# Attention scores in batches of three head pairs, one of them in the output projection's banks, with buffers of one pair

## The chip, the cores and the metric

The kernel runs on one core of a Trainium2 chip. The metric is the device time of one execution in microseconds. The engines of the core work in parallel, each with its own program in order, and wait for one another through semaphores: TensorE (PE; its weight loads are listed apart as PEld), VectorE (DVE), ScalarE (ACT), GpSimd (POOL), and SyncE (SP), which here only issues DMA transfers. TensorE writes to PSUM, which has eight banks of 512 fp32 columns.

## The reference

All tensors are bf16: 2048 tokens of width 640, 32 heads of 192, and a window of the last 512 keys and values. The expert part (B) touches only the two best tokens.

```python
xn = _layernorm(x, axis=-1)
q  = (xn @ wq).reshape(B, Sq, 32, 192)             # heads
scores = einsum("bhqd,bhkd->bhqk", q, k) * 192 ** -0.5   # 512 keys of each head
p  = softmax(scores);  o = einsum("bhqk,bhkd->bhqd", p, v)
s  = o.reshape(B, Sq, 32 * 192) @ wo
# B: r = xn @ w_r picks 2 tokens; their gated FFN, times sigmoid(r), is added to xn there
g  = silu(xn with the two updated rows)
return x + s * g
```

## The kernel before

The heads are taken in 8 groups of four, a group's heads in two pairs. A *step* is a group, a block of 512 tokens (`t5`) and a pair of heads: 64 steps. A *quad* `k` is half a step, 256 tokens of a pair, that is two tiles of 128 tokens (`u`) with two heads each: 128 quads, and 256 *pairs* (a tile of 128 tokens with two heads). For every pair of heads the 384 rows of q and k are three chunks of 128: chunk 0 belongs to the first head, chunk 2 to the second, and chunk 1 holds the last 64 rows of each.

The order of all engines is that in which the program issues the instructions. For the first twelve quads it is written out by hand in a list of tokens (`FIRST`), for the last in another (`LAST`); between them a loop (L797) lays down, for each quad `k`:

- `quad(k)`: scores of two tiles into four PSUM banks (`ps_sc`). First four matmuls with 128 rows (L296, L297: chunks 0 and 2), then four with 64 rows (L302, L303: chunk 1, one head in the upper half of the array and one in the lower);
- four row maxima on VectorE (`row_max`, L314) and four exponentials on ScalarE (`exps`, L321), which also sum each row; then one DMA transpose of the 128x2048 exponentials, pexp to pT (L327, 16 blocks of 128x128);
- the q products of the next step (`q_item`, L263), evicted by ScalarE (L268);
- the o products of quad `k - 2` (`o_products`, L339; two items, one for each tile), scaled on VectorE by the reciprocal sums (L353), and after the second one DMA transpose of the 128x768 o_sb to oT (L357, 6 blocks);
- one item of the output projection (`w_item`) for a tile of tokens that is complete, six quads later: six matmuls of 512 columns (L386) and six of 128 (L388) into one tile of two banks (`ps_w`), added to `s_acc` by VectorE (L394);
- pieces of other work by quad number (`mid` and `bg`): loads of the next group's weights, keys and values, issued by SyncE, the transposes of keys (L125, 12 blocks), the expert's part, and the final load of x (L780).

PSUM holds two banks for q and o products (`ps_f`), two for w and four for scores. Buffers rotate: two of pexp and four of pT, each for a quad, two of o_sb, three of oT. All DMA transposes are on SyncE's queue.

LayerNorm of the first 512 tokens uses ScalarE's square root; for the others VectorE computes 1 / deviation by three Newton steps (`rsqrt_newton`, L182), and the row statistics with `bn_stats` (L418).

The functions that the diff touches, and what calls them, with the profile's line numbers:

Of the kernel before, what the change touches and what calls it, by code (L numbers as in the profile page):

```python
# [21 lines left out]
def kernel(ctx, tc, A_x, A_k_cache, A_v_cache, A_wq, A_wo, B_x, B_w_r, B_w_gate, B_w_up, B_w_down, out):  # L22
# [45 lines left out]
    p_pool = pool("p", 2)  # L68
    pT_pool = pool("pT", 4)
    o_pool = pool("o", 2)  # L70
    oT_pool = pool("oT", 3)
# [70 lines left out]
    warm_ps = ps_w.tile([P, W], FP32, name="warm_ps", tag="w_ps")  # L142
# [62 lines left out]


# [17 lines left out]
    def k_turn(copies):  # L224

        grp[0]["kT"] = kT_pool.tile([P, PAIRS, NJ, 3, P], BF16, name="kT")
        tp = ps_w.tile([P, NJ * 3, P], BF16, name="tp_k", tag="w_ps")
        kp = grp[0][("k", 0)].rearrange("p j h d -> p (j h d)")
        kT = grp[0]["kT"][:, 0].rearrange("p j c t -> p (j c) t")
        step = NJ * 3 // len(copies)  # L230
        for c in range(NJ * 3):
            nc.tensor.transpose(out=tp[:, c, :], in_=kp[:, c * P:(c + 1) * P], identity=ident)
        for q, copy in enumerate(copies):
            cs = slice(q * step, (q + 1) * step)
            copy(out=kT[:, cs], in_=tp[:, cs])
# [10 lines left out]
    NH = 2 * NS  # L246
# [3 lines left out]
    pe_of = {}  # L250
# [34 lines left out]
    def quad(k):  # L285
        i, hf = divmod(k, 2)
        g, t5, pr = steps[i]
        qT = qT_of[i]
        kT = grp[g]["kT"]
        kp = kT[:, pr]  # L290
        tiles = []
        for u in range(2):
            ssl = slice((2 * hf + u) * P, (2 * hf + u + 1) * P)
            s0 = ps_sc.tile([P, W], FP32, name="s0", tag="sc")
            s1 = ps_sc.tile([P, W], FP32, name="s1", tag="sc")
            nc.tensor.matmul(s0, lhsT=qT[:, 0, ssl], rhs=kp[:, :, 0, :], start=True, stop=False)  # L296
            nc.tensor.matmul(s1, lhsT=qT[:, 2, ssl], rhs=kp[:, :, 2, :], start=True, stop=False)  # L297
            tiles.append((s0, s1))
        for u in range(2):
            ssl = slice((2 * hf + u) * P, (2 * hf + u + 1) * P)  # L300
            s0, s1 = tiles[u]
            nc.tensor.matmul(s0, lhsT=qT[0:64, 1, ssl], rhs=kp[0:64, :, 1, :], start=False, stop=True)  # L302
            nc.tensor.matmul(s1, lhsT=qT[64:128, 1, ssl], rhs=kp[64:128, :, 1, :], start=False, stop=True)  # L303
        return tiles
# [3 lines left out]
    def row_max(k, tiles, c):  # L308
        if c == 0:
            nm_of[k] = small.tile([P, 4], FP32, name="nm")  # L310
            l_of[k] = small.tile([P, 4], FP32, name="lsum", bufs=6)
            pT_of[k] = pT_pool.tile([P, 2, 2, NJ, P], BF16, name="pT")
            pe_of[k] = p_pool.tile([P, 2, 2, W], BF16, name="pexp")
        nc.vector.tensor_reduce(out=nm_of[k][:, c:c + 1], in_=tiles[c // 2][c % 2], axis=AX.X, op=ALU.max, negate=True)  # L314

    def exps(k, u, tiles):
        pexp = pe_of[k]
        nm = nm_of[k]
        for hh in range(2):
            c = 2 * u + hh  # L320
            nc.scalar.activation(out=pexp[:, u, hh, :], in_=tiles[u][hh], func=ACT.Exp, bias=nm[:, c:c + 1],  # L321
                                 scale=1.0, accum_out=l_of[k][:, c:c + 1])
        if k >= NH - 2:
            nc.sync.dma_start_transpose(out=pT_of[k][:, u].rearrange("p h j t -> p (h j) t"),
                                        in_=pexp[:, u].rearrange("p h k -> p (h k)"))
        elif u == 1:
            nc.sync.dma_start_transpose(out=pT_of[k].rearrange("p u h j t -> p (u h j) t"),  # L327
                                        in_=pexp.rearrange("p u h k -> p (u h k)"))

    def recip(k):  # L330
        nc.vector.reciprocal(out=l_of[k], in_=l_of[k])

    def o_products(k, u):
        i, hf = divmod(k, 2)
        g, t5, pr = steps[i]
        o_ps = f_tile([P, 2, Dh], FP32, "o_ps")
        for hh in range(2):
            for j in range(NJ):
                nc.tensor.matmul(o_ps[:, hh, :], lhsT=pT_of[k][:, u, hh, j, :], rhs=grp[g]["v"][:, 2 * pr + hh, j, :],  # L339
# [3 lines left out]
    def o_scaled(k, u, o_ps, act=False):  # L343
        i, hf = divmod(k, 2)
# [566 lines left out]
```

## Time and profile before

| | us |
|---|---|
| median of 3 runs | 814.38 |
| lowest, highest | 813.56, 817.44 |
| the profiled execution | 815.97 |
| its span | 814.2 |
| PE busy in the span | 796.1 |
| DVE busy | 625.4 |
| ACT busy | 485.6 |
| POOL busy | 208.2 |

Lines of the profile name the source line, the engine, the operation, output and inputs, tile sizes and a count; then the busy time and the mean of one in ns; then idle time of the engine before such instructions and what ended most of it. SyncE has no row of busy time: its entries are seen in its timeline, "SPq", with the time that one took. In a timeline a row that stands for several instructions carries the time from the first's start to the last's end.

### The profile page before, as it was taken

What the parts mean: (1) busy time and instruction counts of PE and PEld (TensorE: products, weight loads), DVE (VectorE), ACT (ScalarE), POOL (GpSimd) and SP (SyncE); (2) the same over time, 40 slices, a digit from 0 to 9 for tenths busy, and PEclk for the clock granted to TensorE, in tenths of its full rate; (3) what the DMA queues carried; (4) which work ended last, traced back from release to release, by engine and by line L of the source; (5) the groups of instructions that cost most, each with busy time, mean ns of one, the idle gap of its engine ahead of it and who ended that gap; (6) DMA issues with size and microseconds to landing.
All of it is one profiled execution on the core that took longest, in us unless ns stands there. A gap on an engine that the chain in (4) does not pass through costs nothing. (4 is left out here: it accounts for less than half of the span.)

```text
span 814.2 us, 15365 instructions
## 1 busy us (share of the span) xinstructions
PE 796.1 (98%) x5715; PEld 446.1 (55%) x5782; DVE 625.4 (77%) x1249; ACT 485.6 (60%) x1271; POOL 208.2 (26%) x157
## 2 busy tenths in 40 slices
PE   8889999999999999999999999999999999999997
PEld 4455555555555555555555555555555555555555
DVE  7988688887778777677776776777888877767886
ACT  5677666565566556555655565666776765655652
POOL 0001000000000000000001799999920001452533
PEclk9999999999999999999999999999999999999999
DMA  7988999989989999999999999788998879988884
GB/s 233 170 161 170 187 173 192 174 158 191 158 165 163 188 199 191 183 189 180 201 190 193 174 172 195 154 145 148 189 177 151 158 145 197 198 156 156 179 159 117
DMA packets 440555, 142.09 MB, mean 175 GB/s; under 512 B 413572, under 2 KB 440072, under 8 KB 440480
## 3 DMA queue, kind: packets, MB, share of 16 engines
q1 hardware_dynamic: 438720, 138.26, 89.9%
q0 software_dynamic: 816, 2.03, 1.0%
q8 instruction: 45, 0.74, 0.4%
q10 hardware_dynamic: 944, 0.82, 0.3%
q14 instruction: 30, 0.25, 0.1%
HBM read 39.98 MB, written 2.62 MB: 52 GB/s over the span
## 5 line engine op out<-in xcount | busy, mean ns | idle before, releaser
L321 ACT ACTIVATE pexp<-s,nm 128x512 bf16<-128x512 f32 x512 | 348.3, 691 | 253.8 <-DVE nm L314 163.4
L314 DVE TENSOR_REDUCE nm<-s 128x1 f32<-128x512 f32 x512 | 319.0, 683 | 55.2 <-PE s L303 55.2
L263 PE MATMUL q_ps<-xnT,wq_g 128*128 128x512 bf16 x945 | 234.9, 380 | 0.6 <-DMA xnT<-xn 0.6
L339 PE MATMUL o_ps<-v_sb,pT 128*128 128x192 bf16 x2048 | 210.3, 246 | 2.3 <-DMA pT<-pexp 0.8
L339 PEld LDWEIGHTS <-pT 128*128 128x128 bf16 x2048 | 173.0, 98 | 49.5 <-issue 5.8
L353 DVE TENSOR_TENSOR o_sb<-o_ps,lsum 128x384 bf16<-128x384 f32 x248 | 135.2, 545 | 47.2 <-PE o_ps L339 47.1
L386 PE MATMUL w_ps<-wo_g,oT 128*128 128x512 bf16 x662 | 163.4, 379 | 3.4
L263 PEld LDWEIGHTS <-wq_g 128*128 128x128 bf16 x945 | 80.2, 98 | 119.6 <-issue 50.1
L268 ACT ACTIVATE qT<-q_ps 128x512 bf16<-128x512 f32 x185 | 109.9, 596 | 40.8 <-PE q_ps L263 40.6
L394 DVE TENSOR_TENSOR s_acc<-s_acc,w_ps 128x640 f32<-128x640 f32 x96 | 78.9, 821 | 61.5 <-PE w_ps L388 61.4
L321 ACT ACTIVATION_READ_ACCUMULATOR pexp<-s,nm 128x1 f32 x512 | 106.3, 208 | 0.0
L386 PEld LDWEIGHTS <-oT 128*128 128x128 bf16 x726 | 69.1, 98 | 57.1
L297 PE MATMUL s<-kT,qT 128*128 128x512 bf16 x256 | 97.0, 379 | 1.9 <-ACT pexp L321 1.2
L296 PE MATMUL s<-kT,qT 128*128 128x512 bf16 x256 | 97.1, 379 | 0.6 <-ACT pexp L321 0.6
L303 PE MATMUL s<-kT,qT 64*128 64x512 bf16 x256 | 77.1, 381 | 0.0
L302 PE MATMUL s<-kT,qT 64*128 64x512 bf16 x256 | 77.1, 381 | 0.0
L388 PEld LDWEIGHTS <-oT 128*128 128x128 bf16 x726 | 50.7, 98 | 28.6
L725 POOL TENSOR_SCALAR yh<-y_bc,oh 128x640 bf16<-128x640 bf16 x32 | 60.3, 1884 | 3.4 <-DMA y_bc<-y_d 1.9
L388 PE MATMUL w_ps<-wo_g,oT 128*128 128x128 bf16 x726 | 60.3, 219 | 0.0
L711 POOL DMA_DIRECT2D y<-yp x4 | 2.1, 530 | 219.4 <-DMA oT<-o_sb 219.4
L726 POOL TENSOR_TENSOR xn<-xn,yh 128x640 bf16<-128x640 bf16 x32 | 44.7, 1396 | 2.7
L302 PEld LDWEIGHTS <-qT 64*128 64x128 bf16 x256 | 14.1, 94 | 56.3 <-issue 56.3
(135 smaller groups left out, 388.6 us busy)
## 6 DMA issues: line engine op xcount, KB each, us to landing
wo_g<-in_A_wo_dram SPq DMA_DIRECT2D x48, 160.0 KB, 2.9
wq_g<-in_A_wq_dram SPq DMA_DIRECT2D x35, 192.0 KB, 3.0
k_raw<-in_A_k_cache_dram SPq DMA_DIRECT2D x32, 192.0 KB, 3.1
v_sb<-in_A_v_cache_dram SPq DMA_DIRECT2D x32, 192.0 KB, 2.8
x_fin<-in_A_x_dram SPq DMA_DIRECT2D x16, 160.0 KB, 2.7
pT<-pexp SPq DMA_TRANSPOSE x130, 4.8
oT<-o_sb SPq DMA_TRANSPOSE x126, 3.2
wgu<-in_B_w_gate_dram SPq DMA_DIRECT2D x15, 128.0 KB, 2.9
```

The lines of the kernel that those rows point to most:

```text
L263: nc.tensor.matmul(q_ps, lhsT=grp[g]["wq"][:, dc, col0:col0 + P], rhs=xnT[:, t5 * 4:(t5 + 1) * 4, dc, :], start=(dc == 0), stop=(dc == DC ...
L268: nc.scalar.activation(out=qT_of[i][:, c, :], in_=q_ps, func=ACT.Copy, scale=scale)
L296: nc.tensor.matmul(s0, lhsT=qT[:, 0, ssl], rhs=kp[:, :, 0, :], start=True, stop=False)
L297: nc.tensor.matmul(s1, lhsT=qT[:, 2, ssl], rhs=kp[:, :, 2, :], start=True, stop=False)
L302: nc.tensor.matmul(s0, lhsT=qT[0:64, 1, ssl], rhs=kp[0:64, :, 1, :], start=False, stop=True)
L314: nc.vector.tensor_reduce(out=nm_of[k][:, c:c + 1], in_=tiles[c // 2][c % 2], axis=AX.X, op=ALU.max, negate=True)
L321: nc.scalar.activation(out=pexp[:, u, hh, :], in_=tiles[u][hh], func=ACT.Exp, bias=nm[:, c:c + 1], scale=1.0, accum_out=l_of[k][:, c:c + 1])
L339: nc.tensor.matmul(o_ps[:, hh, :], lhsT=pT_of[k][:, u, hh, j, :], rhs=grp[g]["v"][:, 2 * pr + hh, j, :], start=(j == 0), stop=(j == NJ - 1))
L353: nc.vector.tensor_tensor(out=o_sb[:, u], in0=o_ps, in1=l_of[k][:, 2 * u:2 * u + 2].unsqueeze(2).to_broadcast([P, 2, Dh]), op=ALU.mult)
L386: nc.tensor.matmul(w_ps[:, 0:DA], lhsT=oT[:, c // 3, u % 2, c % 3, :], rhs=wo_g[:, c, 0:DA], start=(c == 0), stop=(c == CPG - 1))
L388: nc.tensor.matmul(w_ps[:, DA:D], lhsT=oT[:, c // 3, u % 2, c % 3, :], rhs=wo_g[:, c, DA:D], start=(c == 0), stop=(c == CPG - 1))
L394: nc.vector.tensor_tensor(out=s_acc[:, n, :], in0=s_acc[:, n, :], in1=w_ps, op=ALU.add)
```

## The change

The unit of work becomes the pair. Buffers of pexp, pT, o_sb and oT hold one pair each (4, 6, 3 and 14 of them), and each pair has DMA transposes of its own: 128x1024 of exponentials, 128x384 of o. After the first twelve units, which are quads as before, a unit is three pairs: `scores(U)` issues six matmuls with 128 rows and then six with 64 rows. Two of the three pairs go to the four banks of `ps_sc`, the first pair to the two banks of the output projection (`w_banks`), which are two tiles of one bank now. The last unit is one pair. `w_item` computes two halves of 320 columns, one in each bank, with an eviction each.

The loop's order is a list (`STRETCH`), with o products one unit behind their scores. `FIRST` and `LAST` are written anew. For later tokens, 1 / deviation comes from ScalarE's Ln and Exp and one Newton step (`rsqrt_parts`), for four of the tiles of tokens (those that `FIRST` lists with `sa`) the row statistics come from ScalarE sums (`rows`), and a table set with both functions is loaded where a warming Exp stood.

The core of the diff:

```diff
-    p_pool = pool("p", 2)
-    pT_pool = pool("pT", 4)
-    o_pool = pool("o", 2)
-    oT_pool = pool("oT", 3)
+    p_pool = pool("p", 4)
+    pT_pool = pool("pT", 6)
+    o_pool = pool("o", 3)
+    oT_pool = pool("oT", 14)
...
+    def rsqrt_parts(var_ap, out_ap):
+
+        T = {}
+
+        def ln():
+            T["v"] = small.tile([P, 4], FP32, name="nw_v")
+            T["a"] = small.tile([P, 4], FP32, name="nw_a")
+            nc.scalar.activation(out=T["a"], in_=var_ap, func=ACT.Ln, bias=eps_t[:, 0:1], scale=1.0)
+
+        def ex():
+            nc.scalar.activation(out=out_ap, in_=T["a"], func=ACT.Exp, scale=-0.5)
+
+        def v():
+            nc.gpsimd.tensor_scalar(out=T["v"], in0=var_ap, scalar1=EPS, scalar2=None, op0=ALU.add)
+
+        def s1():
+            nc.vector.scalar_tensor_tensor(out=T["a"], in0=out_ap, scalar=-0.5, in1=out_ap, op0=ALU.mult, op1=ALU.mult)
+
+        def s2():
+            nc.vector.tensor_tensor(out=T["a"], in0=T["a"], in1=T["v"], op=ALU.mult)
+
+        def s3():
+            nc.vector.scalar_tensor_tensor(out=out_ap, in0=T["a"], scalar=1.5, in1=out_ap, op0=ALU.add, op1=ALU.mult)
+        return [ln, ex, v, s1, s2, s3]
...
+    HEAD = 12
+    units = [[2 * k, 2 * k + 1] for k in range(HEAD)]
+    while units[-1][-1] < NM - 2:
+        units.append([units[-1][-1] + 1 + a for a in range(3)])
+    units.append([NM - 1])
+    NU = len(units)
...
+    def w_banks():
+
+        if not wb:
+            wb.extend(ps_w.tile([P, W], FP32, name=f"w_{c}", tag=f"w{c}") for c in range(2))
+        return wb
+
+    def scores(U):
+
+        ms = units[U]
+        tiles = {}
+        for m in ms[1:] + ms[:1] if len(ms) == 3 else ms:
+            g, t5, pr = steps[m // 4]
+            ssl = slice((m % 4) * P, (m % 4 + 1) * P)
+            if len(ms) == 3 and m == ms[0]:
+                s0, s1 = w_banks()
+            else:
+                s0 = ps_sc.tile([P, W], FP32, name="s0", tag="sc")
+                s1 = ps_sc.tile([P, W], FP32, name="s1", tag="sc")
+            qT, kp = qT_of[m // 4], grp[g]["kT"][:, pr]
             nc.tensor.matmul(s0, lhsT=qT[:, 0, ssl], rhs=kp[:, :, 0, :], start=True, stop=False)
             nc.tensor.matmul(s1, lhsT=qT[:, 2, ssl], rhs=kp[:, :, 2, :], start=True, stop=False)
-            tiles.append((s0, s1))
-        for u in range(2):
-            ssl = slice((2 * hf + u) * P, (2 * hf + u + 1) * P)
-            s0, s1 = tiles[u]
+            tiles[m] = (s0, s1)
+        for m in ms:
+            g, t5, pr = steps[m // 4]
+            ssl = slice((m % 4) * P, (m % 4 + 1) * P)
+            s0, s1 = tiles[m]
+            qT, kp = qT_of[m // 4], grp[g]["kT"][:, pr]
             nc.tensor.matmul(s0, lhsT=qT[0:64, 1, ssl], rhs=kp[0:64, :, 1, :], start=False, stop=True)
             nc.tensor.matmul(s1, lhsT=qT[64:128, 1, ssl], rhs=kp[64:128, :, 1, :], start=False, stop=True)
-        return tiles
+        return [tiles[m] for m in ms]
 
     nm_of = {}
 
-    def row_max(k, tiles, c):
+    def row_max(U, tiles, c):
         if c == 0:
-            nm_of[k] = small.tile([P, 4], FP32, name="nm")
-            l_of[k] = small.tile([P, 4], FP32, name="lsum", bufs=6)
-            pT_of[k] = pT_pool.tile([P, 2, 2, NJ, P], BF16, name="pT")
-            pe_of[k] = p_pool.tile([P, 2, 2, W], BF16, name="pexp")
-        nc.vector.tensor_reduce(out=nm_of[k][:, c:c + 1], in_=tiles[c // 2][c % 2], axis=AX.X, op=ALU.max, negate=True)
-
-    def exps(k, u, tiles):
-        pexp = pe_of[k]
-        nm = nm_of[k]
+            nm_of[U] = small.tile([P, 6], FP32, name="nm")
+            l_of[U] = small.tile([P, 6], FP32, name="lsum", bufs=6)
+        nc.vector.tensor_reduce(out=nm_of[U][:, c:c + 1], in_=tiles[c // 2][c % 2], axis=AX.X, op=ALU.max, negate=True)
...
+    def exps(U, a, tiles):
+        m = units[U][a]
+        unit_of[m] = (U, a)
+        pT_of[m] = pT_pool.tile([P, 2, NJ, P], BF16, name="pT")
+        pexp = p_pool.tile([P, 2, W], BF16, name="pexp")
...
+            c = 2 * a + hh
+            nc.scalar.activation(out=pexp[:, hh, :], in_=tiles[a][hh], func=ACT.Exp, bias=nm_of[U][:, c:c + 1],
+                                 scale=1.0, accum_out=l_of[U][:, c:c + 1])
+        nc.sync.dma_start_transpose(out=pT_of[m].rearrange("p h j t -> p (h j) t"), in_=pexp.rearrange("p h k -> p (h k)"))
...
+    def o_scaled(m, o_ps, act=False, turn=True):
+        U, a = unit_of[m]
+        o_of[m] = o_pool.tile([P, 2, Dh], BF16, name="o_sb")
+        oT_of[m] = oT_pool.tile([P, 3, P], BF16, name="oT")
+        ls = l_of[U][:, 2 * a:2 * a + 2]
         if act:
             for hh in range(2):
-                nc.scalar.activation(out=o_sb[:, u, hh], in_=o_ps[:, hh, :], func=ACT.Copy, scale=l_of[k][:, 2 * u + hh:2 * u + hh + 1])
+                nc.scalar.activation(out=o_of[m][:, hh], in_=o_ps[:, hh, :], func=ACT.Copy, scale=ls[:, hh:hh + 1])
         else:
-            nc.vector.tensor_tensor(out=o_sb[:, u], in0=o_ps, in1=l_of[k][:, 2 * u:2 * u + 2].unsqueeze(2).to_broadcast([P, 2, Dh]), op=ALU.mult)
-        if pr == 0 and u == 0:
-            oT_of[(g, t5, hf)] = oT_pool.tile([P, PAIRS, 2, 3, P], BF16, name="oT")
-        if u == 1 and k < NH - 2:
-            nc.sync.dma_start_transpose(out=oT_of[(g, t5, hf)][:, pr].rearrange("p u c t -> p (u c) t"),
-                                        in_=o_sb.rearrange("p u h d -> p (u h d)"))
-
-    def o_item(k, u, act=False):
-        return lambda: o_scaled(k, u, o_products(k, u), act)
-
-    def o_turn(k):
-
-        i, hf = divmod(k, 2)
-        g, t5, pr = steps[i]
-        tp = tail_banks[0].tile([P, 2, 3, P], BF16, name="tp_o", tag="t")
-        for u in range(2):
-            o2 = o_of[k][:, u].rearrange("p h d -> p (h d)")
+            nc.vector.tensor_tensor(out=o_of[m], in0=o_ps, in1=ls.unsqueeze(2).to_broadcast([P, 2, Dh]), op=ALU.mult)
+        if turn:
+            nc.sync.dma_start_transpose(out=oT_of[m], in_=o_of[m].rearrange("p h d -> p (h d)"))
...
+    def w_products(b, u, w_ps, part, off=0):
+
+        wo_g = grp[steps[b * PAIRS][0]]["wo"]
+        for c in range(CPG):
+            nc.tensor.matmul(w_ps[:, part.start - off:part.stop - off], lhsT=oT_of[8 * b + 4 * (c // 3) + u][:, c % 3, :],
+                             rhs=wo_g[:, c, part], start=(c == 0), stop=(c == CPG - 1))
...
+            for h, w_ps in enumerate(w_banks()):
+                cs = slice(h * HD, (h + 1) * HD)
+                w_products(b, u, w_ps, cs, cs.start)
+                if g == 0 and act:
+                    nc.scalar.copy(out=s_acc[:, n, cs], in_=w_ps[:, 0:HD])
+                elif g == 0:
+                    nc.vector.tensor_copy(out=s_acc[:, n, cs], in_=w_ps[:, 0:HD])
+                elif g < NG - 1:
+                    nc.vector.tensor_tensor(out=s_acc[:, n, cs], in0=s_acc[:, n, cs], in1=w_ps[:, 0:HD], op=ALU.add)
+                else:
+                    if h == 0:
+                        t = fin_pool["t"].tile([P, D], FP32, name="fin_t")
+                        o = fin_pool["o"].tile([P, D], BF16, name="fin_o")
+                    nc.vector.tensor_tensor(out=t[:, cs], in0=w_ps[:, 0:HD], in1=xn[:, n, cs], op=ALU.mult)
...
-            nc.scalar.activation(out=const.tile([P, 1], FP32, name="warm"), in_=eps_t, func=ACT.Exp)
+            nc.scalar.preload_act_table_set("natural_log_exp_and_others")
...
+    STRETCH = "M0 M1 R O1 E0 q1 M2 M3 E1 O1 M4 M5 E2 W1 m q1 n W q O b".split()
...
+    for U in range(HEAD, NU - 2):
+        ms = units[U]
+        qs = [q_item(*divmod(n, 3)) for n in range(nq, q_until(U - HEAD))]
+        nq += len(qs)
+        os_ = [o_item(m) for m in range(no, ms[0])]
+        no += len(os_)
+        ws = []
+        while 12 + 2 * nw <= ms[-1]:
+            ws.append(w_item(*divmod(nw, 4)))
+            nw += 1
+        ks = [m // 2 for m in ms if m % 2 == 0]
+        todo = {"q": qs, "O": os_, "W": ws, "m": mid.pop(ks[0], []), "b": bg.pop(ks[-1], []),
+                "n": bg.pop(ks[0], []) + mid.pop(ks[-1], []) if len(ks) > 1 else []}
+        tiles = scores(U)
+        for token in STRETCH:
+            if token[0] == "M":
+                row_max(U, tiles, int(token[1]))
+            elif token[0] == "E":
+                exps(U, int(token[1]), tiles)
+            elif token[0] == "R":
+                if U > HEAD:
+                    recip(U - 1)
+            elif token[1:] == "":
+                while todo[token]:
+                    todo[token].pop(0)()
+            else:
+                for f in todo[token[0]][:int(token[1])]:
+                    todo[token[0]].pop(0)()
+        assert not any(todo.values())
```

## The prediction

> **What bounds the kernel now.** I read the page first, then the windows by stage, then the timeline of TensorE and of SyncE in the middle of the run, then the views of SyncE's transposing lines. The page:
>
> ```profile
> span 814.2 us, 15365 instructions
> PE 796.1 (98%) x5715; PEld 446.1 (55%) x5782; DVE 625.4 (77%) x1249; ACT 485.6 (60%) x1271; POOL 208.2 (26%) x157
> PE   8889999999999999999999999999999999999997
> L302 PEld LDWEIGHTS <-qT 64*128 64x128 bf16 x256 | 14.1, 94 | 56.3 <-issue 56.3
> ```
>
> TensorE is the bound. Only the first slices show holes. The last line counts 128 stops (one per batch of scores) before the 64-row weights. The timeline shows what a stop is:
>
> ```profile
> 403.12 0.38 PE L297 MATMUL s<-kT,qT 128*128 128x512 bf16 x1
> 403.44 0.39 PE L302 MATMUL s<-kT,qT 64*128 64x512 bf16 x1
> 403.44 0.39 PE L303 MATMUL s<-kT,qT 64*128 64x512 bf16 x1
> 403.66 0.38 PE L302 MATMUL s<-kT,qT 64*128 64x512 bf16 x1
> 403.67 0.38 PE L303 MATMUL s<-kT,qT 64*128 64x512 bf16 x1
> 403.97 1.25 PE L263 MATMUL q_ps<-xnT,wq_g 128*128 128x512 bf16 x5
> ```
>
> Matmuls of 512 columns start 0.215 us apart. From the last 128-row score to the first 64-row one it is 0.32, and from the last 64-row one to the next product 0.31: 0.10 + 0.09 = 0.19 us lost per batch, on the path.
>
> The second resource is not in the page's busy rows: SyncE, which issues every transpose and nearly every load in order. Its timeline where it has no pause:
>
> ```profile
> 304.84 2.91 SPq L327 DMA_TRANSPOSE pT<-pexp  x1
> 307.85 1.23 SPq L357 DMA_TRANSPOSE oT<-o_sb  x1
> 309.13 0.57 SPq L120 DMA_DIRECT2D wo_g<-in_A_wo_dram  x1
> 309.75 1.31 SPq L626 DMA_DIRECT2D wgu<-in_B_w_gate_dram  x2
> 311.17 2.91 SPq L327 DMA_TRANSPOSE pT<-pexp  x1
> ```
>
> The next instruction begins 0.05 us after a transpose ends, or 0.10 if it is a transpose (a separate wait instruction stands between). An entry starts only after its data is there: the pT at 573.24, after a pause of 1.2 us, begins just as ScalarE has read out the sum of its batch's last exponential. So these durations hold no waiting for data; in them SyncE can do nothing else. How they go with size (min/median/max ns):
>
> ```profile
> L327 SPq DMA_TRANSPOSE pT<-pexp x126: 1317/2536/4295, 18.4 to 786.5; - x126
> ...
> L125 SPq DMA_TRANSPOSE kT<-k_raw x15: 1279/1922/3092, 10.1 to 689.5; - x15
> ...
> L324 SPq DMA_TRANSPOSE pT<-pexp x4: 1232/1240/1302, 790.6 to 797.1; - x4
> ...
> L357 SPq DMA_TRANSPOSE oT<-o_sb x126: 1212/1273/2653, 31.1 to 799.0; - x126
> ```
>
> These are 16, 12, 8 and 6 blocks of 128x128. The minima are nearly one number: 1.15 us for the instruction and 0.0105 us per block. What the median of 16 blocks has above its minimum is waiting for the DMA engines to drain.
>
> **The change part by part.**
>
> *Batches of three.* Batches go from 128 to 90 (12 of two pairs, 77 of three, 1 of one). 38 x 0.19 = 7.2 us less on TensorE. The count of matmuls for scores, q and o stays.
>
> *w in halves.* These rows are its price on TensorE:
>
> ```profile
> 806.29 1.79 PE L859 MATMUL w_t<-wo_g,oT 128*128 128x512 bf16 x12
> 807.92 1.79 PE L859 MATMUL w_e<-wo_g,oT 128*128 128x320 bf16 x12
> ```
>
> The first is six matmuls of 512 and six of 128, the second twelve of 320: the same 1.79 us, so nothing. On VectorE an eviction goes from 0.82 us to two of 0.49 (the row fin_t<-w_e): +0.16 x 121 = 19 us, hidden, since VectorE is busy 77%.
>
> *The w banks shared with scores.* A w product now waits until a pair's exponentials have left those two banks, and scores of the next batch wait until w is evicted. Walked from the first score at 0, with row maxima 0.60 us apart (four in 2.48): first maximum 1.81, both exponentials of that pair done 3.96; TensorE reaches the first w at 2.15 + 0.66 + 1.08 + 0.66 = 4.55. Its evictions stand behind the sixth maximum, the first from 6.48 to 6.97; TensorE reaches the second w of a stretch (every other one has two) at 7.26. Both fit, the second by 0.3 us: nothing. If VectorE comes later by more than that, about 38 stretches pay up to 0.35 us, 13 us at most.
>
> *LayerNorm of later tokens.* Each of three Newton chains (12 VectorE steps near 0.16 us) becomes Ln, Exp (nearest row: the Sqrt of 128x1, 0.30 us) and one step; eight row sums move to ScalarE at about 0.74 us each (the tanh of 128x640). It touches only the first 100 us, where TensorE is idle 6.6 us between 20 and 100 (73.4 busy of 80). Ends: 6.6 us gained or as much lost. I take 1 gained. One more activation table load (1.28 us each in this trace) comes before the first tanh, on an engine busy 60%: nothing.
>
> *Buffers of one pair.* This decides. Each transpose of pexp or o_sb is cut in two: 130 + 126 become 256 pT of 8 blocks and 254 oT of 3 blocks, all on SyncE. Bytes and blocks stay, instructions double. Eight blocks: 1.24 us, a row. Three blocks are in no row. The line through the minima gives 1.18; from below the nearest row is a plain copy, 0.43 (wo_g); from above the median of six blocks, 1.27. I take 1.18, since 6 and 8 blocks differ by 0.02 and 16 blocks by 0.1.
>
> SyncE's program from pair 24's pT to pair 255's (by the order of the changed program): 231 pT x (1.24 + 0.10) = 309.5; 231 oT x (1.18 + 0.10) = 295.7; 14 kT x 1.45 = 20.3; 182 loads, at their medians of 0.43 to 0.59 plus 0.055, = 104. Sum 729.5 us, 3.16 per pair. TensorE's own pace over it: pair 24's exponentials are done at about 92 now, and pair 255's pT starts at 797.1, 705 us, less 7 for the batches: 698, 3.02 per pair. So SyncE becomes slower than TensorE by 31 us. Queued behind it are the pT on which o products wait. These now come one batch after their exponentials (before, two batches), so a late transpose stops TensorE at the first o of a stretch; scores and q stand behind that, in order.
>
> The sum: 92 - 1 + 729.5 = 820.5, pair 255's transpose. After it 3.2 to landing (the median of those four), o 0.7, oT of pair 254 landed about 7.0, two w of 1.63 and the 4.5 us that now follow the last matmul: 14.8, end at 835. Add 3 us where SyncE has few loads and TensorE leads again (the last 32 pairs, about 0.1 each) and 6 for draining: the median of six blocks lies 0.06 above its minimum, taken on 231 oT is 14, and I take not quite half, because 11 blocks now come per 3.16 us while 22 alone pass in about 3.7 (555.45 to 559.16 in the timeline). Span 844. The profiled run took 815.97 for a span of 814.2, and lies 1.6 above the median of 814.38, so the time is forecast at 844.
>
> [...]
>
> **The rivals.**
>
> *Issue time goes with the blocks (faster).* Place: oT on SyncE. For it: 16 blocks have a median of 2.54 us and 8 blocks 1.24, exactly half; then 3 blocks take half of 1.27, 0.64. Against it: 6 blocks cost what 8 do, and 16 have been issued in 1.32. SyncE then needs 729.5 - 231 x 0.54 = 605 us, TensorE stays the bound, and the gain of 7.2 + 1 stands: 814.4 - 8 = 806. It decides from below 1.04 us per oT (1.18 - 31/231).
>
> *Nearly balanced.* oT at 1.0 us: SyncE's mean is 0.04 under TensorE's pace, but its loads are bunched (stretches with the expert's weights ask 3.2 to 3.5 us per pair even so), and a lag is one batch deep. Some 8 of the 16-pair stretches lose 1 to 3 us: 806 + 8 = 814.
>
> *SyncE bound and draining too.* 8 blocks at 1.30 (the largest of the four) and 3 at 1.27: + 231 x 0.15 = 35, less the 6 already in: 873. For it: half of the pT now wait on draining. Against: SyncE itself then issues slower.
>
> *The w banks collide* (13 us, above): hidden while SyncE is the bound; without it 819.
>
> **How the numbers follow.** SyncE bound 0.80 (its own range 828 to 866), draining too 0.04, w banks 0.02, balanced 0.04, faster rival 0.10. About 0.5% is what a measurement of this kernel can tell from no change (810.3 to 818.5). Faster takes the 0.10, same the balanced case at 0.04, slower the rest, 0.86. The predicted time is 844; the range of 805 to 868 reaches down to the faster rival, whatever an oT costs below 1.04, and up to 8 and 3 blocks at 1.29 and 1.24; it leaves out the draining one.
>
> **What would show it.** Right: oT of 128x384 on SyncE with a minimum near 1.18 us; SyncE without pauses from about 100 us on; TensorE idle 30 to 45 us in all, ended by pT at the o products; 90 stops before 64-row weights instead of 128; VectorE and ScalarE waiting for TensorE. Wrong: oT under 1.0 us, pauses on SyncE, TensorE at 99.5 us of 100 as now. The step most likely to fail is the price of three blocks, extended from rows of six and more. Next is the head.

## The result and the profile after

The changed kernel takes 906.63 us (median of 4 runs, 904.60 to 908.86) against 814.41 us for the kernel before on the same chip: a ratio of 1.1118, 95% interval 1.1097 to 1.1140. It is 92 us slower where 30 were forecast, above the range of 805 to 868. The profiled run took 905.68 us for a span of 903.9. Of the four runs of loads_pool below one (957.79 us) was in a slower state of the chip and is left out of its time.

The page of the changed kernel, with its totals, TensorE's busy tenths and granted clock, and its dearest row (busy, mean of one, then the idle time ahead of it and what ended that):

```profile
span 903.9 us, 16427 instructions
PE 816.7 (90%) x5776; PEld 494.0 (55%) x5776; DVE 633.8 (70%) x1304; ACT 498.1 (55%) x1281; POOL 216.4 (24%) x175
...
PE   8898889996999888998879997999988998799997
...
PEclk9999998999999899999989998999999999899999
...
L376 PE MATMUL o_ps<-v_sb,pT 128*128 128x192 bf16 x2048 | 220.0, 253 | 67.8 <-DMA pT<-pexp 63.4
```

TensorE was 98% busy and is 90% busy now. The holes lie all along the run, and most of them stand ahead of the o products and end when a transpose of the exponentials lands. What TensorE and its weight loads waited for (us in all, times, longest):

```profile
PE o_ps L376 <- DMA pT<-pexp: 63.4, 34, 5.2
...
PEld L376 <- DMA pT<-pexp: 85.5, 46, 5.7
PEld L344 <- issue: 38.5, 89, 0.9
```

The stops ahead of the 64-row weights went from 128 to 89, as the batches of three were to make them. SyncE's rows for its three transposes (minimum, median and maximum in ns; 8, 12 and 3 blocks):

```profile
L365 SPq DMA_TRANSPOSE pT<-pexp x256: 1231/1253/2373, 17.7 to 888.5; - x128
...
L125 SPq DMA_TRANSPOSE kT<-k_raw x15: 1273/1904/2237, 10.7 to 772.3; - x15
...
L391 SPq DMA_TRANSPOSE oT<-o_sb x254: 1177/1214/2526, 28.0 to 892.7; - x127
```

Three blocks have their minimum at 1.18 us, where the prediction put it, and hardly less than eight. SyncE's timeline in the middle of the run (start, duration, line, transfer):

```profile
499.24 1.22 SPq L391 DMA_TRANSPOSE oT<-o_sb  x1
500.56 1.26 SPq L365 DMA_TRANSPOSE pT<-pexp  x1
501.92 1.22 SPq L391 DMA_TRANSPOSE oT<-o_sb  x1
503.19 0.57 SPq L110 DMA_DIRECT2D wq_g<-in_A_wq_dram  x1
503.85 1.99 SPq L391 DMA_TRANSPOSE oT<-o_sb  x1
505.94 2.63 SPq L365 DMA_TRANSPOSE pT<-pexp  x2
```

Here SyncE never pauses: each instruction begins 0.05 to 0.1 us after the one ahead of it. Summed over its timeline from pair 24's transposed exponentials (98.9 us) to pair 255's (888.5), SyncE is without work for 4 of 790 us; in the kernel before it was for 81 of 703. The transposes queue up: from the moment ScalarE has read out the last sum of a transpose's exponentials to the issue of that transpose, a median of 3.81 us passes (longest 10.7), against 0.03 us in the kernel before.

The windows from 100 to 800 us, before and after (length, busy time of TensorE, weight loads, VectorE, ScalarE and GpSimd, then clock, share of the DMA engines, GB/s):

```profile
100.00:800.00 700.00, 695.25 (x5009) 390.35 (x5067) 536.86 (x1028) 417.33 (x1101) 193.43 (x133) 1.00 0.94 175
```

```profile
100.00:800.00 700.00, 633.70 (x4479) 385.69 (x4478) 478.27 (x976) 381.11 (x975) 158.52 (x102) 0.97 0.80 156
```

Every engine does less in the same time, and so do the DMA engines, 0.80 instead of 0.94. What has become the bound is not in these rows: it is the queue that issues.

### The profile page after: what moved, and what is told of

It is laid out like the page before. It is cut to its first block, busy times and chain, and to the rows that moved or that the text cites. A ratio compares the mean times of both kernels' runs of the same rounds, so it can differ in the third digit from the quotient of the medians.

```text
span 903.9 us, 16427 instructions
## 1 busy us (share of the span) xinstructions
PE 816.7 (90%) x5776; PEld 494.0 (55%) x5776; DVE 633.8 (70%) x1304; ACT 498.1 (55%) x1281; POOL 216.4 (24%) x175
## 5 line engine op out<-in xcount | busy, mean ns | idle before, releaser
L376 PE MATMUL o_ps<-v_sb,pT 128*128 128x192 bf16 x2048 | 220.0, 253 | 67.8 <-DMA pT<-pexp 63.4
L363 ACT ACTIVATE pexp<-s,nm 128x512 bf16<-128x512 f32 x358 | 242.4, 684 | 32.8 <-ACT pexp L363 15.3
L363 ACT ACTIVATE pexp<-w,nm 128x512 bf16<-128x512 f32 x154 | 104.5, 683 | 235.2 <-DVE nm L354 127.4
L354 DVE TENSOR_REDUCE nm<-s 128x1 f32<-128x512 f32 x358 | 228.9, 681 | 4.7 <-PE s L345 3.8
L410 PE MATMUL w<-wo_g,oT 128*128 128x320 bf16 x1500 | 227.0, 301 | 3.9 <-DVE s_acc L426 1.8
L410 PEld LDWEIGHTS <-oT 128*128 128x128 bf16 x1536 | 150.4, 99 | 65.5 <-issue 6.6
L354 DVE TENSOR_REDUCE nm<-w 128x1 f32<-128x512 f32 x154 | 99.1, 686 | 60.6 <-PE w L345 60.4
L428 DVE TENSOR_TENSOR s_acc<-s_acc,w 128x320 f32<-128x320 f32 x192 | 86.6, 481 | 26.3 <-PE w L410 26.1
L363 ACT ACTIVATION_READ_ACCUMULATOR pexp<-s,nm 128x1 f32 x358 | 71.9, 201 | 0.0
L336 PE MATMUL s<-kT,qT 128*128 128x512 bf16 x179 | 67.9, 379 | 1.8 <-DMA kT<-k_raw 1.2
L337 PE MATMUL s<-kT,qT 128*128 128x512 bf16 x179 | 67.9, 379 | 1.8 <-ACT pexp L363 0.9
L345 PE MATMUL s<-kT,qT 64*128 64x512 bf16 x179 | 53.2, 377 | 0.0
L344 PE MATMUL s<-kT,qT 64*128 64x512 bf16 x179 | 53.2, 377 | 0.0
```

What stands on the lines that cost most here:

```text
L354: nc.vector.tensor_reduce(out=nm_of[U][:, c:c + 1], in_=tiles[c // 2][c % 2], axis=AX.X, op=ALU.max, negate=True)
L363: nc.scalar.activation(out=pexp[:, hh, :], in_=tiles[a][hh], func=ACT.Exp, bias=nm_of[U][:, c:c + 1], scale=1.0, accum_out=l_of[U][:, c:c ...
L376: nc.tensor.matmul(o_ps[:, hh, :], lhsT=pT_of[m][:, hh, j, :], rhs=grp[g]["v"][:, 2 * pr + hh, j, :], start=(j == 0), stop=(j == NJ - 1))
L410: nc.tensor.matmul(w_ps[:, part.start - off:part.stop - off], lhsT=oT_of[8 * b + 4 * (c // 3) + u][:, c % 3, :], rhs=wo_g[:, c, part], sta ...
L428: nc.vector.tensor_tensor(out=s_acc[:, n, cs], in0=s_acc[:, n, cs], in1=w_ps[:, 0:HD], op=ALU.add)
```

## The experiments

The theory: SyncE issues one DMA after the other, a transpose costs it some 1.2 us however few blocks it has, and twice the transposes no longer fit into TensorE's time. Its rivals: batches of three and the w banks carry the loss; the moved blocks do; the delay of a transpose does, not the rate.

### One part of the change at a time, in the kernel before

split_pT issues the transpose of the exponentials for each pair, split_oT that of the scaled o, split_both does both:

```diff
-        if k >= NH - 2:          # split_pT, split_both: the exponentials
+        if True:
...
-        if u == 1 and k < NH - 2:      # split_oT, split_both: the scaled o
-            nc.sync.dma_start_transpose(out=oT_of[(g, t5, hf)][:, pr].rearrange("p u c t -> p (u c) t"),
-                                        in_=o_sb.rearrange("p u h d -> p (u h d)"))
+        if k < NH - 2:
+            nc.sync.dma_start_transpose(out=oT_of[(g, t5, hf)][:, pr, u], in_=o_sb[:, u].rearrange("p h d -> p (h d)"))
```

> The kernel before with one edit: the transpose of the exponentials is issued for each pair of heads (8 blocks) instead of for two pairs at once (16 blocks). Everything else is the kernel before. Theory, SyncE's issue time is the limit: in the kernel before SyncE stood idle for 81 us of the 703 us between pair 24's and pair 255's transpose of the exponentials. The edit replaces 114 issues of 2.486 us in that stretch (283 us) by 231 of 1.326 us (306 us, the mean of the changed kernel) and adds about 115 gaps of 0.1 us, +35 us in all, which fits into the 81 us: no change, 814 us (810 to 822). Rival, every extra transpose costs its time on the path: 129 x 1.25 = +160 us. Rival, what slows the changed kernel is not the issue of transposes but its order in batches of three pairs: 814 us here as well, so this run tells the first rival apart, not this one.

> The kernel before with one edit: the transpose of the scaled o is issued for each pair (3 blocks) instead of for two pairs at once (6 blocks). Theory, SyncE's issue time is the limit: 115 issues of 1.479 us (170 us) become 231 of 1.257 us (290.5 us), with 115 more gaps of 0.1 us: +132 us on SyncE, of which 81 us fill its idle time and 51 us lengthen the span: about 865 us (850 to 880). Rival, the batches of three pairs or the scores in the banks of o wo are what slows the changed kernel: 814 us here. Rival, the transfers themselves (blocks moved) are the limit: the blocks are the same as before, so 814 us.

> The kernel before with both edits, one pair in each transpose of the exponentials and of the scaled o, as the changed kernel has them, but with the order, the batches of two pairs, the o wo products in 512 and 128 columns and the Newton steps of the kernel before. Theory, SyncE's issue time is the limit: 35 + 132 - 81 = +86 us by the terms of the two single edits, 900 us (885 to 915), most of the changed kernel's 906.6. Rival, the batches of three pairs, the scores in the banks of o wo or the waits between them carry the loss: 814 to 830 us here.

Measured: split_pT 815.02 us (ratio 0.9998, 0.9988 to 1.0008), split_oT 905.02 us (1.1111, 1.1088 to 1.1133), split_both 904.46 us (1.1110, 1.1074 to 1.1145). One line of the change, o transposed for each pair, brings the whole loss, without batches of three, shared banks or halves. Its timeline on SyncE:

```profile
498.22 3.02 SPq L327 DMA_TRANSPOSE pT<-pexp  x1
501.32 2.50 SPq L357 DMA_TRANSPOSE oT<-o_sb  x2
503.88 0.83 SPq L110 DMA_DIRECT2D wq_g<-in_A_wq_dram  x1
504.81 2.86 SPq L327 DMA_TRANSPOSE pT<-pexp  x1
507.76 2.50 SPq L357 DMA_TRANSPOSE oT<-o_sb  x2
```

For two pairs this is 3.0 us of exponentials and 2 x 1.25 of o. In split_pT the 16-block transposes become two of 8 and take nearly as long together: 231 x 1.321 = 305 us in place of 114 x 2.486 = 283. So 16 blocks already cost almost what 2 x 8 do, and 6 blocks cost about what 3 do (medians of 1.273 us in the kernel before and 1.206 here): splitting the one adds little to the queue (split_both is no slower than split_oT), splitting the other nearly doubles it. split_oT came out 40 us above its expectation. Its 16-block transposes take 2.683 us instead of 2.486 (114 x 0.197 = 22 us), because that price was the mean of a queue with pauses: in the kernel before, the 16-block transposes behind a pause took 2.13 us on average and the others 2.92. Its 3-block ones take 1.322 instead of 1.257 (231 x 0.065 = 15 us); that price came from the changed kernel, a queue without pauses too, and why they are longer here is not shown.

### The halves of o wo

whalf puts the halves of 320 columns into the kernel before, both in one tile; whalf2 gives each half a tile of its own, as the changed kernel does:

```diff
+            w_ps = ps_w.tile([P, 2, W], FP32, name="w_ps")          # whalf
+            w_ps = [ps_w.tile([P, W], FP32, name=f"w_ps{h}", tag=f"w{h}") for h in range(2)]   # whalf2
...
+            for h in range(2):
+                cs = slice(h * HD, (h + 1) * HD)
+                for c in range(CPG):
+                    nc.tensor.matmul(w_ps[h][:, 0:HD], lhsT=oT[:, c // 3, u % 2, c % 3, :], rhs=wo_g[:, c, cs], ...)
...
+                    nc.vector.tensor_tensor(out=s_acc[:, n, cs], in0=s_acc[:, n, cs], in1=w_ps[h][:, 0:HD], op=ALU.add)
```

> The kernel before with one edit: o wo in two halves of 320 columns with an eviction after each half, as the changed kernel has it (the batches, buffers and transposes stay). Theory: 2 x 6 x 0.136 = 1.63 us of products for each tile of 128 tokens against 6 x (0.216 + 0.056) = 1.63 us, so TensorE is level, and VectorE's second eviction lies in its idle time: 814 us (810 to 822). Rival: the halves cost the changed kernel some of its 92 us, in which case this run is above 825.

> The kernel before with o wo in halves of 320 columns in two tiles of one bank each, as the changed kernel has them, where the run whalf had both halves in one tile of two banks. Theory: what slowed whalf (927.9 us) was a wait of the second half's products for the first half's eviction, since both lie in one tile (TensorE's weights and products of o wo waited 96 us for VectorE's evictions there, 3.9 us in the changed kernel); with two tiles the halves cost nothing: 814 us (810 to 822). Rival, the halves themselves or the second eviction cost time: above 830 us, in which case the halves also stand in the changed kernel's 92 us.

Measured: whalf 927.94 us (1.1389, 1.1370 to 1.1408), whalf2 816.00 us (0.9994, 0.9980 to 1.0008). TensorE's waits in whalf:

```profile
PE w_ps L388 <- DVE s_acc L394: 65.2, 96, 1.6
PE w_ps L388 <- DVE s_acc L392: 18.7, 13, 1.9
PE w_ps L388 <- DVE fin_t L399: 6.3, 9, 1.6
```

Of these 90 us nothing is left with two tiles. The halves themselves cost nothing. Halves of one tile made the products wait for evictions, 118 times in these three rows, and that belongs to the run whalf alone.

### One part undone in the changed kernel

merge_oT keeps the whole change but transposes the scaled o of two pairs at once:

```diff
+        if m % 2 == 0:
+            o2_of[m] = (o_pool.tile([P, 2, 2, Dh], BF16, name="o_sb"), oT_pool.tile([P, 2, 3, P], BF16, name="oT"))
+        o2, oT2 = o2_of[m - m % 2]
+        o_of[m], oT_of[m] = o2[:, m % 2], oT2[:, m % 2]
...
+        if m < NM - 4 and m % 2:
+            nc.sync.dma_start_transpose(out=oT2.rearrange("p u c t -> p (u c) t"), in_=o2.rearrange("p u h d -> p (u h d)"))
```

> The changed kernel with one edit: the scaled o of pairs 2i and 2i + 1 lies in one buffer and is transposed by one instruction of 6 blocks; only the last four pairs keep theirs. Batches of three pairs, scores in the banks of o wo, halves of 320 columns and the one-pair transposes of the exponentials all stay, and as many blocks are moved. Theory, SyncE's issue time of the o transposes is the limit: 231 issues of 1.257 us and their gaps (290.5 + 23 us) become 115 of 1.31 us and theirs (151 + 12 us), 151 us off the 786 us that SyncE worked between pair 24's and pair 255's transpose, which leaves 635 us; TensorE then sets the time, about 700 us there: 806 to 822 us, 812 in the middle. Rival, the batches of three or the scores in the banks of o wo carry part of the loss: well over 830 us. Rival, the blocks moved are the limit: 906 us as before.

Measured: 814.69 us (0.9978, 0.9965 to 0.9991). The loss is gone, with the same blocks moved, so blocks are not the limit. SyncE has 72 us of pauses again. The rest of the change is worth 1.9 us here, not the 8 predicted, because TensorE still waits a little, as merge_late below bears out:

```profile
PE o_ps L377 <- DMA pT<-pexp: 6.5, 9, 1.6
```

lag2 leaves the transposes alone and gives them a whole batch more time:

```diff
-    pT_pool = pool("pT", 6)
+    pT_pool = pool("pT", 8)
...
-    oT_pool = pool("oT", 14)
+    oT_pool = pool("oT", 13)
...
-        os_ = [o_item(m) for m in range(no, ms[0])]
+        os_ = [o_item(m) for m in range(no, units[U - 1][0])]       # and LAST to match
```

> The changed kernel with one edit: the o products stand two batches of three pairs behind the scores instead of one (8 buffers of transposed exponentials instead of 6, 13 instead of 14 of transposed o), so that every transpose has about 9 us more to land. Theory, SyncE's issue time is the limit: it is a rate, not a delay, and the same instructions are issued: 906 us (900 to 915), with the idle time of TensorE ended by something else or merely later. Rival, the delay from the exponentials through the queue to the o products is the limit, so that earlier work would cover it: 815 to 850 us.

Measured: 906.22 us (1.1094, 1.1068 to 1.1119). Nothing is gained; SyncE pauses for 4.7 of 791 us. TensorE's waiting moved one step down the chain, to the transposed o ahead of o wo:

```profile
PE w L410 <- DMA oT<-o_sb: 55.7, 22, 6.8
```

More distance between issue and use helped against a delay (6.5 us of waits became 0.9 in merge_late below); against a queue that is slower than its consumers it only chose where they wait (63.4 us ahead of the o products in the changed kernel, 55.7 ahead of o wo here).

### What a transpose costs a queue

micro runs transposes alone, of 1 to 24 blocks, back to back.

> No part of the reference is computed and zeros are written: only SyncE's transposes run, one behind the other from one buffer into four in turn: 30 each of 1, 3, 6, 8 and 16 blocks, 15 of 24 blocks, then 20 times 3 and 8 blocks in turn, then 20 times 3 blocks, a load of 192 KB, and 8 blocks. By the fit that the prediction used (1.15 us + 0.0105 us a block) one takes 1.16, 1.18, 1.21, 1.23, 1.32 and 1.40 us. Rival, from the 2.68 us of the 16-block and the 1.32 us of the 8-block transposes in the runs split_oT and split_pT: a floor of 1.2 us up to some 7 blocks and about 0.165 us a block above: 1.2, 1.2, 1.2, 1.3, 2.65 and 4.0 us. Transposes in turn with loads: the fit expects nothing more; draining would show as over 1.3 us behind a load.

Measured medians: 1.25 us for 1 block, 1.25 for 3, 1.29 for 6, 1.33 for 8, 2.40 for 16 and 3.70 for 24. Neither line of the expectation fits throughout, and the rival's is the nearer: a floor to 8 blocks, then about 0.15 us a block. The windows for 3, 8, 16 and 24 blocks (length, VectorE, GpSimd, clock, DMA share, GB/s):

```profile
45.00:82.00 37.00, 0.00 (x0) 0.00 (x0) 1.00 0.31 62
...
125.00:164.00 39.00, 0.00 (x0) 0.00 (x0) 1.00 1.00 191
168.00:238.00 70.00, 0.00 (x0) 0.00 (x0) 1.00 1.14 211
244.00:294.00 50.00, 0.00 (x0) 0.00 (x0) 1.00 1.12 209
```

So at 3 blocks the DMA engines are busy for a third of the time and the issue is the limit; at 8 both are level; above, the engines are full (16 and 24 blocks move the same, some 210 GB/s) and the issue waits for them. In turn, 3 and 8 blocks take 1.262 and 1.307 us. A load of 192 KB (0.58 us) between them lengthens a turn from 2.67 to 3.20 us (medians), although the DMA engines have room for it, with a share of 0.77: the queue adds up what it issues.

In micro a transpose cost more than a plain transfer: at 3 blocks a transpose of 96 KB takes its queue 1.25 us and a load of 192 KB 0.58, and at 16 blocks, with the engines full, transposes move 211 GB/s, while the one large plain transfer of micro, 2560 KB written at its end, landed in 9.1 us, some 288 GB/s.

### The long transposes

In the changed kernel 43 transposes of exponentials and o took 1.45 to 2.53 us, 29 us more than 43 x 1.25, and they come at intervals of some 18 us. The records of the DMA queues show packets of 16 KB on an instruction queue at about that rate; 34 of the 43 overlap with one, of the 467 others only 8. micro_pe sets the transposes beside a TensorE stream and nothing else:

```diff
+    for _ in range(3000):
+        nc.tensor.matmul(acc, lhsT=z[:, 0, 0:P], rhs=z[:, 1, 0:320], start=True, stop=True)
+    for _ in range(150):
+        turn(3, "y3")
+        turn(8, "y8")
```

> No part of the reference is computed and zeros are written: SyncE issues 150 times a transpose of 3 and one of 8 blocks in turn (in the run micro these took 1.262 and 1.307 us, none above 1.32), while TensorE runs 3000 matmuls of 320 columns with a weight load each, some 410 us. Theory, a packet of instructions holds transposes up: about one packet of 16 KB each 17 us, and a transpose of 1.5 to 2.5 us at most of them, 15 to 25 in all, the rest as in micro. Rival, the long transposes of the changed kernel come from loads and from the transposes' own queue: no transpose above 1.4 us here, whatever the packets do.

SyncE's row and the instruction queue's (packets, MB, share) in that run:

```profile
L40 SPq DMA_TRANSPOSE y<-x_in x300: 1178/1307/2517, 5.3 to 420.5; - x150
```

```profile
q8 instruction: 23, 0.38, 0.4%
```

There are 23 packets and 23 transposes of 1.57 to 2.52 us, and each packet overlaps with one of these; the medians stay at 1.261 and 1.307 us. In micro, which has no work for TensorE and no such queue, none of the 3- and 8-block transposes took more than 1.35. So the packets come with TensorE's stream, on a queue that the page calls instruction and that takes 0.4% of the DMA engines, and the 34 transposes of the changed kernel that met one took some 0.76 us more than 1.25 each. What lengthened the 9 others of the changed kernel is open; the 34 make up 26 of the 29 us.

### Other ways to relieve SyncE

oT_act lets ScalarE issue every third o transpose, loads_pool lets GpSimd issue the loads:

```diff
-            nc.sync.dma_start_transpose(out=oT_of[m], in_=o_of[m].rearrange("p h d -> p (h d)"))      # oT_act
+            (nc.scalar if m % 3 == 2 else nc.sync).dma_start_transpose(out=oT_of[m], in_=o_of[m].rearrange("p h d -> p (h d)"))
...
-            bg[k1 + dc].append(lambda g=g, dc=dc: wq_piece(g + 1, dc, nc.sync))        # loads_pool, and five lines like it
+            bg[k1 + dc].append(lambda g=g, dc=dc: wq_piece(g + 1, dc, nc.gpsimd))
```

> The changed kernel with one edit: the o transpose of every third pair is issued by ScalarE instead of SyncE. Count, size and order of the transposes stay. Theory, the limit is the time in which SyncE alone can issue: 77 of its 231 o transposes between pair 24 and pair 255 leave it, 77 x (1.257 + 0.10) = 104 us of its 786, which leaves 681 us, less than the 700 us that TensorE needs there; ScalarE takes some 85 x 1.26 = 107 us more and is busy 55% now, and each such transpose stands behind VectorE's o ahead of the next batch's exponentials: 815 to 840 us. Rival, what costs 1.25 us is not the issuing queue but something that all transposes share, whoever issues them: 900 to 910 us. What the merged run alone could not tell apart is this.

> The changed kernel with one edit: the loads of keys, values and weights for later groups and experts are issued by GpSimd instead of SyncE (166 of the 182 loads between pair 24 and pair 255). All 462 one-pair transposes stay on SyncE. Theory, the limit is the sum of what SyncE issues one after the other: 97 us of loads and 8 us of gaps leave its 786 us, 681 us remain, less than TensorE's 700: 812 to 830 us. Rival, the limit is something that only the transposes use (462 of them at some 1.29 us, in whatever queue): the loads then hid beside it and moving them changes nothing, 900 to 910 us. Rival, the loads take as long to prepare on GpSimd as to make keys or weights late: between the two, with TensorE waiting for them.

Measured: oT_act 1137.22 us (1.3917, 1.3864 to 1.3970), loads_pool 946.04 us (1.1614, 1.1567 to 1.1660). Neither theory gave these numbers, and neither run settles its question. What SyncE waited for in oT_act, and its row of exponentials in loads_pool:

```profile
SPq L391 <- DMA oT<-o_sb: 285.3, 77, 6.2
```

```profile
L365 SPq DMA_TRANSPOSE pT<-pexp x256: 1231/1257/7328, 16.5 to 928.4; - x128
```

In oT_act SyncE waits ahead of an o transpose until an earlier one has landed, 77 times and 3.7 us each, 285 us in all where the run lost 231 to the changed kernel, whose waits on SyncE have no such row. The run shows the price of that wait, not its reason. ScalarE pays too: it waits ahead of 77 of its 85 transposes, some 380 us in all (9.5 the longest), and exponentials stand behind it in its program; TensorE waits 141 us for those ahead of o wo. What the run adds otherwise is that ScalarE's issues of 3 blocks took 1.21 us on average (minimum 1.19), so the floor is not SyncE's alone. In loads_pool 97 us of loads are gone from SyncE, but between pair 24 and pair 255 its transposes take 88 us more (364 + 313 + 33 for exponentials, o and keys, against 306 + 291 + 26), it waits 17 us for keys and pauses for 38. The 62 transposes of exponentials with a packet of GpSimd's queue inside them took 2.21 us on average, the 194 others 1.35. The time taken off the queue came back as longer issues.

### A version that beats both

merge_lag2 and merge_q1 tried to remove the 6.5 us of waits that merge_oT had left, the first with the o products a batch later, the second with the first q product ahead of the first o product:

```diff
-        os_ = [o_item(m) for m in range(no, ms[0])]
+        os_ = [o_item(m) for m in range(no, units[U - 1][0])]       # merge_lag2, with 7 and 7 buffers
...
-    STRETCH = "M0 M1 R O1 E0 q1 M2 M3 E1 O1 M4 M5 E2 W1 m q1 n W q O b".split()
+    STRETCH = "M0 M1 R q1 O1 E0 M2 M3 E1 O1 M4 M5 E2 W1 m q1 n W q O b".split()       # merge_q1
```

> The run merge_oT with the o products two batches of three pairs behind the scores (7 buffers of transposed exponentials, 7 of transposed o for two pairs each). In merge_oT TensorE was idle 9.7 us between 100 and 800 us against 4.7 in the kernel before, 6.5 of it for late transposes of the exponentials, which eats most of the 7.2 us that 38 fewer batches save. Theory: with SyncE no longer the limit the wait is a delay, and 9 us more of slack remove it: 807 to 812 us. Rival, the seven buffers or the o transposes before o wo make a wait of the same size: 814 us. Rival, the savings of the batches were never there: 814 us with TensorE idle under 5 us.

> The run merge_oT with one more edit: in each batch the first q product stands ahead of the first o product. That gives the transposed exponentials 1.08 us more (five products of 512 columns at 0.216 us) before the o products that waited for them 9 times, 6.5 us in all, 1.6 us at most. Theory: 4 to 6 of these 6.5 us go, 809 to 812 us. Rival: ScalarE's eviction of q now stands ahead of the exponentials and makes them late by some 0.6 us a batch, which comes back as the same wait or as scores that wait for their banks: 814 to 825 us.

Measured: merge_lag2 886.49 us (1.0855, 1.0818 to 1.0892), merge_q1 848.67 us (1.0400, 1.0386 to 1.0414). Each made a new wait, in the order of the runs:

```profile
PE w L415 <- DMA oT<-o_sb: 60.5, 22, 5.4
```

```profile
ACT qT L301 <- PE q_ps L296: 289.0, 81, 5.1
```

In merge_lag2 the o wo products kept their place and now stand right behind the transpose of the o that they read. In merge_q1 ScalarE, whose program now has q ahead of the exponentials, waits for q, and in some 68 of these 289 us the maximum for the exponentials behind it was ready. merge_late moves the o products by one pair only:

```diff
-        os_ = [o_item(m) for m in range(no, ms[0])]
+        os_ = [o_item(m) for m in range(no, ms[0] - 1)]       # over merge_oT, with 7 and 7 buffers
```

> The run merge_oT with the o products one pair later (7 buffers of transposed exponentials, 7 of transposed o for two pairs each): each transpose has some 3 us more to land, and each o wo product still has at least two pairs between it and the o that it needs, where merge_lag2 left none. Theory: the 6.5 us for which TensorE waited for transposed exponentials go, and the 7.2 us of the batches show: 809 to 812 us, 0.5 to 0.9% under the kernel before. Rival, the margin of o wo is again too small: TensorE waits there for transposed o, 820 to 860 us. Rival, the saving of the batches goes elsewhere: 814 us with TensorE's waits gone.

Measured: 808.28 us (0.9914, 0.9900 to 0.9929), faster than both kernels, if only by 0.9% of the kernel before. TensorE's wait for transposed exponentials and its window from 100 to 800 us:

```profile
PE o_ps L377 <- DMA pT<-pexp: 0.9, 2, 0.5
```

```profile
100.00:800.00 700.00, 696.24 (x5122) 430.54 (x5120) 539.29 (x1109) 431.46 (x1104) 202.74 (x137) 1.00 0.95 175
```

It is the changed kernel but for the o transposes of two pairs, the place of the o products and the number of buffers, and it is 6.9 us under the 815.22 us of the kernel before.

## Why the prediction was right in kind and wrong in size

- **What bounds it.** Right. SyncE's issue of transposes became the bound, the o products waited for transposed exponentials, SyncE had hardly a pause, and the shortest o transpose took 1.18 us. split_oT and merge_oT show it from both sides.
- **SyncE's program, 729.5 us: the step that failed.** It took 789.7, of which 4 were pauses. By kind, measured against the sum: exponentials 231 x (1.326 - 1.24) = +19.8 us; o 231 x (1.257 - 1.18) = +17.9; the key transposes +6 (priced at 1.45 us, though their own row had a median of 1.92); loads 105.6 against some 94, +11.6; gaps as priced. The prices were floors and medians of a queue that often paused, used as means of one that never does. Of the 37.7 us on the two transposes, 27 lie in 38 long ones, most of them of the kind that micro_pe ties to instruction packets; the others had means of 1.261 and 1.210, +11 us.
- **The 9 us allowed (6 for draining, 3 where TensorE leads).** Too small, and the reason given for the 6 fell: the excess is mostly not draining, since the DMA engines' share went down from 0.94 to 0.80.
- **92 - 1 for the head.** Pair 24's transpose was issued at 98.9, 8 us later. The pair's exponentials were done at 94.4 (at 91.2 in the kernel before), and the transpose then stood 4.5 us in the queue: from 28 us on SyncE had less than 1 us of pauses, and the prediction had charged the head with LayerNorm alone. With SyncE relieved it is 90.1 (merge_oT), near the 91 forecast.
- **The sum again.** 98.9 + 789.7 + 15.4 for the tail (14.8 forecast) = 904.0, the span.
- **Batches of three, -7.2 us.** In line with the runs, though hidden in the changed kernel and though no run has the batches alone: 89 stops instead of 128, and merge_late is 6.9 us under the kernel before, which also holds the 1 us of LayerNorm.
- **Halves and w banks, nothing.** Right: whalf2 is level, and TensorE waited 3.5 us for evictions ahead of o wo in the changed kernel. In merge_late, where TensorE sets the time and the shared banks could show, it waited 2.1 us for them.
- **TensorE idle 30 to 45 us.** It was 87 us, 63 of them in the place named. The forecast did not follow from its own sum either: a span of 844 us less some 789 us of products leaves 55.
- **The line 1.15 us + 0.0105 us a block.** Near to 8 blocks, where the medians of micro lie 0.07 us (3 blocks) to 0.10 us (8) above it, and wrong above, where 16 take 2.40 in a queue without pauses. The rival "issue time goes with the blocks" was right above 8 blocks and wrong below, where it had to be right to matter.
- **The rival "SyncE bound and draining too", 873 us at 0.04.** It had the two prices nearly as measured (1.30 and 1.27), for a cause that was mostly another. What no case held were the loads, the key transposes and the head, 26 us together. This rival deserved more than 0.04, and those three terms a price of their own: with 4 us of pauses in place of 81, the queue had no room left for them.

## What to carry to other kernels

Count a queue that issues DMAs as an engine: sum its instructions in one stretch and compare that with the bound's time, and when it comes near, price each instruction with its mean in a stretch without pauses, not with its minimum. Do not cut a transpose below the size at which its transfer takes as long as its issue (8 blocks of 128 x 128 here: 1.33 us in micro with the DMA engines' share at 1.00, against 1.25 us and 0.31 at 3 blocks); above that, smaller buffers cost the queue little, as split_pT (305 us in place of 283) and split_both show. Where a queue is the bound, as here, fewer and larger transfers help (merge_oT, 814.69 us) and longer distances do not (lag2, 906.22); where it is not, the distance must be given to each consumer along the chain, as merge_lag2 (886.49) and merge_late (808.28) show.

## What the runs showed of the hardware

- The queue that the page calls instruction shares the DMA engines with the data (0.4% of them in micro_pe, 0.3% in the changed kernel): packets of 16 KB, 23 in the 431.8 us of micro_pe and 45, some 19 us apart, in the changed kernel. All 23 and 34 of the 45 overlapped with a long transpose; the 34 long transposes of the changed kernel that met one took 26 us more than 34 x 1.25, 0.76 each.
- In the runs in which TensorE waited long, the granted clock was lower. In the changed kernel, with waits of up to 5.2 us, it was 0.972 on average and the products took 816.7 us busy; in merge_late, which has the same number of matmuls and waits of up to 1.9 us, the clock was 1.00 and they took 790.2; in oT_act, with waits of up to 10.7 us, it was 0.898. In the changed kernel TensorE had seven waits over 3 us, and at six of them the granted clock fell to 0.5, five times before the wait ended and once 0.4 us after its end, for 3.4 or 6.8 us. The loss of the changed kernel is not made by it, since SyncE sets the time there: split_oT had 0.989 and took as long (905.02 us).
- In loads_pool, loads on another queue were not free for transposes: GpSimd's queue had 16.5% of the DMA engines, and all 20 transposes over 3 us (up to 7.3) had packets of that queue inside them. Why it costs so much there stays open.
